# Expert products of a routed feed-forward layer, written as pairs of half-width products in TensorE's columns

## The chip, the cores and the metric

The kernel runs on one core of one Trainium2 chip. The metric is the device time of one execution in microseconds (us). The kernel before takes 718.14 us, the median of three runs (717.37 to 718.94). Everything is kept in 32-bit floats except a few masks.

A few words on names. TensorE (PE in the profile) multiplies a *stationary* matrix, loaded first into its array of 128 rows and 128 columns, by a *moving* matrix that is streamed through. In the profile the load is a record LDWEIGHTS of the row "PEld", the stream a record MATMUL of the row "PE". A product that uses only part of the array is told by its size in the records: `128*64` is one that fills all 128 rows and 64 of the columns. Two such products, one in each half of the columns, can be under way at the same time. PSUM is the memory that TensorE writes; the half of the columns used is the half of PSUM's 128 partitions written. VectorE is DVE, ScalarE is ACT, GpSimd is POOL, SyncE is SP.

## The reference, cut to what matters

First a block-sparse attention over 4 x 8 heads of 768 tokens gives `x`, 3072 rows of 512. Then each row goes to one of eight experts (the one whose embedding is nearest in angle), and is multiplied by that expert's two matrices:

```python
N, D, E, F = (3072, 512, 8, 1024)
...
expert_idx = np.argmax(logits, axis=1)
...
for e in range(E):
    mask = expert_idx == e
    ...
    h = np.maximum(x[mask] @ w1[e], 0.0)          # [rows, 512] @ [512, 1024]
    out[mask] = gate_w[mask, None] * (h @ w2[e])  # [rows, 1024] @ [1024, 512]
```

The change touches only these last two products.

## The kernel before

The attention comes first. Its products are 64 x 64 in size, four at a time in the four quarters of the array. Then the rows are grouped by expert into tiles of 128 rows. An *ordinary* tile belongs to one expert; a *mixed* tile holds 64 rows of one expert and 64 of another, and has always been written with `128*64` pairs. The program holds ordinary tiles under a condition on the number of tiles used, so that not all that are written run; in the profile 23 ordinary and 2 mixed tiles run.

The line numbers (L840 and so on) are those of the profile of the kernel before.

```python
P = 128; DM, E, F = 512, 8, 1024
ND, NF = DM // P, F // P          # 4, 8
HG = G // 2                       # 64

def prepare(k, i):                # turns the rows of the next tile
    ...
    for d in range(ND):
        k.nc.tensor.transpose(ps[:, d, :], x[:, d * P:(d + 1) * P], k.ident)      # L825, xg_ps
    k.turned_rows[i] = ring(k, "xgt", i, 2, k.wp, [P, ND, P])
    k.nc.vector.tensor_copy(out=k.turned_rows[i], in_=ps)

def expert_tile(k, i, meanwhile=None):                # an ordinary tile
    ...
    h = ring(k, "h", i, 2, k.wp2, [P, NF, P])
    half = NF // 2
    for f0 in (0, half):
        hp = ring(k, f"hp{f0}", i, 2, k.hps, [P, half, P])
        for f in range(half):
            for d in range(ND):
                nc.tensor.matmul(hp[:, f, :], lhsT=w1[:, d, (f0 + f) * P:(f0 + f + 1) * P], rhs=xt[:, d, :],
                                 start=(d == 0), stop=(d == ND - 1))              # L840
        if f0 == 0:
            nc.scalar.activation(h[:, 0:half], hp, ACT.Relu)                      # L843
            ...
        else:
            nc.vector.tensor_scalar(out=h[:, half:NF], in0=hp, scalar1=0.0, scalar2=None, op0=ALU.max)  # L847
    if i + 1 < NE + NL:
        prepare(k, i + 1)
    yp = ring(k, "yp", i, 1, k.eps, [P, DM])
    for f in range(NF):
        nc.tensor.matmul(yp, lhsT=h[:, f, :], rhs=w2[:, f, :], start=(f == 0), stop=(f == NF - 1))      # L853
    finish(k, i, yp, x, slot)     # scales the rows (DVE, L861) and scatters them to the output (POOL, L862)

def mixed_tile(k, i):                                 # not changed
    ...
    for f0 in (0, half):
        ...
        for d in range(ND):
            for s, (w1, _) in enumerate(weights):
                lanes = slice(HG * s, HG * (s + 1))
                nc.tensor.matmul(hp[lanes, :], lhsT=xt[:, d, lanes], rhs=w1[:, d, f0 * P:(f0 + half) * P],
                                 start=(d == 0), stop=(d == ND - 1))              # L881
    ...     # eight transposes to 128 x 128 (L893), with the four of prepare (L825) among them
    for f in range(NF):
        for s, (_, w2) in enumerate(weights):
            lanes = slice(HG * s, HG * (s + 1))
            nc.tensor.matmul(yp[lanes, :], lhsT=h[:, f, lanes], rhs=w2[:, f, :], start=(f == 0), stop=(f == NF - 1))  # L901
    finish(k, i, yp, x, slot)
```

`fetch` loads the weights of an expert (2 MB for each of its two matrices) into a ring of three buffers for each matrix, ahead of their use. Work left over from routing (ranks at L551 to L553, slots at L640, a count at L464) is put between and into the first expert tiles; its few products use all 128 columns.

Of the kernel before, what the change touches and what calls it, by code (L numbers as in the profile page):

```python
# [19 lines left out]
P = 128  # L20
# [9 lines left out]
ND, NF = DM // P, F // P  # L30
# [2 lines left out]
NE = (EARLY * S - E * (G - 1) + G - 1) // G  # L33
MIX = 2
HG = G // 2
NG = P // BLK
NU = N // G - NE

NL = max((N - NE * G - (HG + 1) * big - low) // G + big + max(low - 2 * MIX, 0) + (min(low, 2 * MIX) + 1) // 2
         for big in range(E + 1) for low in range(E + 1 - big))  # L40
# [208 lines left out]
def load_blocks(k, g, part=None):  # L249
# [5 lines left out]
    for n, src in enumerate((k.k, k.q)):  # L255
        for e in range(NG):
            src_e = src[b, 2 * j + e // 2].rearrange("(n t) (f d) -> f t n d", t=BLK, d=BLK)[e % 2]
# [428 lines left out]
def dispatch_late(k):  # L686
# [13 lines left out]
    nc.vector.scalar_tensor_tensor(out=low, in0=full, scalar=-float(G), in1=cnt, op0=ALU.mult, op1=ALU.add)  # L700
    nc.vector.tensor_scalar(out=low, in0=low, scalar1=-float(HG), scalar2=None, op0=ALU.is_le)
    half = tiny(name="half_e")
# [33 lines left out]
    nc.vector.scalar_tensor_tensor(out=move, in0=end, scalar=float(G), in1=lim, op0=ALU.mult, op1=ALU.subtract)  # L736
    nc.vector.tensor_scalar(out=there, in0=half, scalar1=float(HG), scalar2=-float(HG), op0=ALU.mult, op1=ALU.add)
    nc.vector.scalar_tensor_tensor(out=there, in0=end, scalar=-float(G), in1=there, op0=ALU.mult, op1=ALU.add)
# [16 lines left out]
def ring(k, name, i, n, pool, shape):  # L755

    key = name, i % n
    if key not in k.rings:
        k.rings[key] = pool.tile(shape, F32, name=f"{name}_{i % n}")
    return k.rings[key]  # L760
# [56 lines left out]
def prepare(k, i):  # L817

    x = k.rows[i][0]
    if i == 0:  # L820
        ps = two_banks(k, "first")[:, 0].rearrange("p (d t) -> p d t", d=ND)
    else:
        ps = ring(k, "xg_ps", i, 1, k.eps, [P, ND, P])
    for d in range(ND):
        k.nc.tensor.transpose(ps[:, d, :], x[:, d * P:(d + 1) * P], k.ident)  # L825
    k.turned_rows[i] = ring(k, "xgt", i, 2, k.wp, [P, ND, P])
    k.nc.vector.tensor_copy(out=k.turned_rows[i], in_=ps)


def expert_tile(k, i, meanwhile=None):  # L830
    nc = k.nc
    ((w1, w2),), (x, slot) = k.weights.pop(i), k.rows.pop(i)
    xt = k.turned_rows.pop(i)
# [3 lines that stand above are left out]
        hp = ring(k, f"hp{f0}", i, 2, k.hps, [P, half, P])  # L837
        for f in range(half):
            for d in range(ND):
                nc.tensor.matmul(hp[:, f, :], lhsT=w1[:, d, (f0 + f) * P:(f0 + f + 1) * P], rhs=xt[:, d, :],  # L840
                                 start=(d == 0), stop=(d == ND - 1))
        if f0 == 0:
            nc.scalar.activation(h[:, 0:half], hp, ACT.Relu)  # L843
            if meanwhile:
                meanwhile()
# [4 lines that stand above are left out]
        prepare(k, i + 1)  # L850
    yp = ring(k, "yp", i, 1, k.eps, [P, DM])
    for f in range(NF):
        nc.tensor.matmul(yp, lhsT=h[:, f, :], rhs=w2[:, f, :], start=(f == 0), stop=(f == NF - 1))  # L853
    finish(k, i, yp, x, slot)


def finish(k, i, yp, x, slot):

    nc = k.nc
    y = ring(k, "y", i, 2, k.wp2, [P, DM])  # L860
    nc.vector.tensor_scalar(out=y, in0=yp, scalar1=x[:, DM:XW], scalar2=None, op0=ALU.mult)  # L861
    nc.gpsimd.indirect_dma_start(  # L862
        out=k.out[:, :], out_offset=bass.IndirectOffsetOnAxis(ap=slot, axis=0),
        in_=y[:, :], in_offset=None, bounds_check=N - 1, oob_is_err=False,
    )


def mixed_tile(k, i):
# [7 lines left out]
    for f0 in (0, half):  # L876
        hp = ring(k, f"hp{f0}", i, 2, k.hps, [P, half, P]).rearrange("p f t -> p (f t)")
# [4 lines that stand above are left out]
# [16 lines left out]
# [4 lines that stand above are left out]
# [122 lines left out]
def expert_tiles(n, between=(), first=None):  # L1024
    between = iter(between)
    for i in range(NE + NU):
        if i + 2 == NE:
            for _ in between:
                pass
        fetch(n, i)  # L1030
        if len(parts(i)) == 2:
            mixed_tile(n, i)
        else:
            expert_tile(n, i, first if i == 0 else None)
        next(between, None)
    used = n.nc.values_load(n.used[0:1, 0:1], min_val=0, max_val=NL)
    with ExitStack() as more:
        for i in range(NU, NL):
            more.enter_context(n.tc.If(used > i))
            fetch(n, NE + i)  # L1040
            expert_tile(n, NE + i)
# [125 lines left out]
```

## Time and profile before

| what | number |
|---|---|
| time, median of three runs | 718.14 us |
| the profiled execution, first to last instruction | 719.4 us |
| TensorE clock granted, mean share | 0.987 |
| stretch of the attention | to about 339 us |
| stretch of the expert tiles | about 339 to 707 us |
| LDWEIGHTS records of TensorE | 8308 |
| HBM read, written | 147.62 MB, 16.01 MB |

The profile was taken in an execution of its own, so its span differs a little from the median. A product of 32-bit floats stands in it as two records LDWEIGHTS and two records MATMUL: the first product of an ordinary tile, written as 2 x 4 x 4 = 32 calls, has 64 of each. [...]the distance between the starts of two records, not the duration, is what a product costs in a stream of them. The chain of work that ended last (followed back from the last instruction, at each step to what released it) gives the time that each group added.

### The profile page before, as it was taken

The page shows a single profiled execution, that of the slowest core. Times are in us where ns is not written, and L with a number is a line of the kernel's source. Part 1 is how long each engine was busy: PE and PEld are TensorE (multiplying, and loading weights), DVE is VectorE, ACT ScalarE, POOL GpSimd, SP SyncE. Part 2 cuts the span into 40 slices and gives each one's busy share as a digit, 9 for nine tenths or more (in the row PEclk, how much of TensorE's full clock was granted, in tenths as well). Part 3 has the DMA queues.
Part 4 walks back from the last instruction along what each step waited for, and adds up shares of the span by engine and source line. Part 5 has one row for each costly group of instructions (what it writes and reads, how often), then busy time and mean ns, then how long its engine had stood idle before and what let it go on. Part 6 is the DMA issues. An engine that isn't in the chain of part 4 may idle for free.

```text
span 719.4 us, 19421 instructions
## 1 busy us (share of the span) xinstructions
PE 698.3 (97%) x8308; PEld 447.8 (62%) x8308; DVE 335.0 (47%) x683; ACT 188.5 (26%) x266; POOL 229.0 (32%) x385
## 2 busy tenths in 40 slices
PE   7899999999999999999999999999999999999992
PEld 3585555555555455556777677766576665767771
DVE  6677778777788888776582111111111111111110
ACT  4355554454545544554100000000000000000000
POOL 2225547554754547653601111111111121111110
PEclk9899999999999999999999999999999999999997
DMA  6433333365335947642999998998899998999980
GB/s 111 91 67 69 69 68 68 64 154 113 52 69 126 181 99 224 201 136 82 328 316 400 397 337 325 342 338 303 297 396 398 398 347 305 404 397 401 340 321 23
DMA packets 180808, 164.76 MB, mean 229 GB/s; under 512 B 128284, under 2 KB 128284, under 8 KB 180710
## 3 DMA queue, kind: packets, MB, share of 16 engines
q1 hardware_dynamic: 174950, 149.80, 66.6%
q0 software_dynamic: 4160, 13.39, 4.7%
q8 instruction: 69, 1.13, 0.7%
q10 hardware_dynamic: 1600, 0.20, 0.2%
q14 instruction: 29, 0.24, 0.1%
HBM read 147.62 MB, written 16.01 MB: 227 GB/s over the span
## 4 chain that ended last, share of the span: by engine, by line
PE 87%; DVE 4%; issue 3%; POOL 1%; DMA 1%; ACT 1%; SPq 1%; DVEq 0%; POOLq 0%; ACTq 0%
PE hp L840 21%; PE yp L853 21%; PE sc L353 19%; PE av L374 16%; PE back L409 3%; PE hp L881 2%; PE yp L901 2%; PE back L402 1%; PE xg_ps L825 1%; ACT e L356 1%; DVE kt L269 1%; DVE esum L371 1%; DVE at L380 0%; DMA out_dram<-y,slot_l 0%; DMA kld<-in_k_dram 0%
## 5 line engine op out<-in xcount | busy, mean ns | idle before, releaser
L356 ACT ACTIVATE e<-sc 128x768 f32<-128x768 f32 x192 | 155.7, 811 | 161.5 <-PE sc L353 156.3
L840 PEld LDWEIGHTS hp<-xgt,w 128*128 128x128 f32 x1472 | 167.7, 192 | 10.8 <-issue 10.2
L840 PE MATMUL hp<-xgt,w 128*128 128x128 f32 x1472 | 169.1, 275 | 0.0
L353 PE MATMUL sc<-qt,kt 64*64 64x384 f32 x1536 | 167.6, 489 | 0.0
L374 PE MATMUL av<-e,vld 64*64 64x384 f32 x1536 | 162.1, 491 | 2.3 <-DVE at L380 2.0
L853 PE MATMUL yp<-w,h 128*128 128x512 f32 x368 | 162.0, 593 | 0.1
L371 DVE TENSOR_TENSOR esum<-esum,e 128x768 f32<-128x768 f32 x128 | 130.9, 1023 | 44.0 <-ACT e L356 42.2
L853 PEld LDWEIGHTS yp<-w,h 128*128 128x128 f32 x368 | 68.0, 190 | 77.5 <-issue 76.3
L437 POOL TENSOR_TENSOR sq<-sq 128x192 f32<-128x192 f32 (+1 forms) x186 | 103.2, 555 | 13.9
L862 POOL DMA_INDIRECT out_dram<-y,slot_l x20 | 20.2, 1009 | 246.0 <-DVE y L861 233.9
L374 PEld LDWEIGHTS av<-e,vld 64*64 64x64 f32 x1536 | 58.6, 134 | 58.7 <-issue 26.7
L843 ACT ACTIVATE h<-hp 128x512 f32<-128x512 f32 x23 | 13.7, 597 | 298.3 <-PE hp L840 284.4
L353 PEld LDWEIGHTS sc<-qt,kt 64*64 64x64 f32 x1536 | 64.7, 135 | 37.3 <-issue 34.2
L861 DVE TENSOR_SCALAR y<-yp,xg 128x512 f32<-128x512 f32 x25 | 18.8, 750 | 140.7 <-PE yp L853 128.2
L847 DVE TENSOR_SCALAR h<-hp 128x512 f32<-128x512 f32 x23 | 15.9, 691 | 131.3 <-PE hp L840 131.3
L353 PE MATMUL sc<-qmask,kmask 64*64 64x384 bf16 x768 | 71.6, 327 | 1.0 <-DVE qmask L167 1.0
L433 POOL TENSOR_TENSOR sq<-x 128x384 f32<-128x384 f32 x31 | 27.0, 873 | 121.7 <-DVE part L422 108.5
L353 PEld LDWEIGHTS <-kmask 64*64 64x64 bf16 x768 | 27.9, 108 | 32.2 <-issue 31.3
L369 DVE TENSOR_TENSOR esum<-e 128x768 f32<-128x768 f32 x32 | 31.1, 973 | 11.5 <-ACT e L356 10.8
L409 PE MATMUL back<-ones,esum 64*64 64x1 f32 x1536 | 27.5, 192 | 0.0
L409 PEld LDWEIGHTS back<-ones,esum 64*64 64x64 f32 x1536 | 26.6, 137 | 0.0
L780 POOL DMA_INDIRECT xg<-x_dram,slot_l x22 | 22.6, 1026 | 6.7 <-issue 6.7
(193 smaller groups left out, 364.1 us busy)
## 6 DMA issues: line engine op xcount, KB each, us to landing
w<-in_moe_w_dram SPq DMA_DIRECT2D x54, 2048.0 KB
w<-in_moe_w_dram SPq DMA_DIRECT2D x16, 512.0 KB
x_dram<-x SPq DMA_DIRECT2D x24, 256.5 KB
vld<-in_v_dram SPq DMA_DIRECT2D x32, 192.0 KB
kld<-in_k_dram SPq DMA_DIRECT2D x60, 96.0 KB
qld<-in_q_dram SPq DMA_DIRECT2D x60, 96.0 KB
x_early<-x SPq DMA_DIRECT2D x12, 256.5 KB
ticks<-dens SPq DMA_DIRECT2D x32, 0.0 KB
```

What stands on the lines that cost most here:

```text
L353: nc.tensor.matmul(ps[D * r:D * (r + 1), h, 0:HALF], lhsT=rows[D * h:D * (h + 1), keys], rhs=cols[D * h:D * (h + 1), queries], start=first ...
L356: k.exps = nc.scalar.activation(e, ps[:, :, 0:HALF], ACT.Exp, scale=SCALE)
L369: k.summed = nc.vector.tensor_tensor(out=k.esum, in0=k.first, in1=e, op=ALU.add)
L371: k.summed = nc.vector.tensor_tensor(out=k.esum, in0=k.esum, in1=e, op=ALU.add)
L374: nc.tensor.matmul(k.av[D * h:D * (h + 1), r, 0:HALF], lhsT=v[D * r:D * (r + 1), h, kc, :], rhs=e[D * r:D * (r + 1), h, :], start=(kc == 0 ...
L409: nc.tensor.matmul(sums[D * s:D * (s + 1), t, h, r:r + 1], lhsT=esum[D * r:D * (r + 1), h, cols], rhs=k.ones[D * r:D * (r + 1), 0:1], star ...
L433: nc.gpsimd.tensor_tensor(out=sq, in0=x, in1=x, op=ALU.mult)
L437: k.squared = nc.gpsimd.tensor_tensor(out=out, in0=sq[:, :, 0:width], in1=sq[:, :, width:2 * width], op=ALU.add).ins
L780: k.nc.gpsimd.indirect_dma_start(out=x[:, :], out_offset=None, in_=(k.x_dram if late else k.x_early)[:, :], in_offset=bass.IndirectOffsetO ...
L840: nc.tensor.matmul(hp[:, f, :], lhsT=w1[:, d, (f0 + f) * P:(f0 + f + 1) * P], rhs=xt[:, d, :], start=(d == 0), stop=(d == ND - 1))
L853: nc.tensor.matmul(yp, lhsT=h[:, f, :], rhs=w2[:, f, :], start=(f == 0), stop=(f == NF - 1))
L862: nc.gpsimd.indirect_dma_start(out=k.out[:, :], out_offset=bass.IndirectOffsetOnAxis(ap=slot, axis=0), in_=y[:, :], in_offset=None, bounds ...
```

## The change: half-width pairs in ordinary tiles

Each product of an ordinary tile that filled the array with 128 stationary columns becomes two products of 64 stationary columns, which write the lower and the upper half of the partitions of the same PSUM tile. The moving operand is the same for both. It is meant to let the two halves of the array load and multiply independently of each other, so that a stationary operand of half the width is loaded in each half at the same time. The mixed tiles, the transposes, the loads of weights and the other engines' work are as they were.

```diff
 HG = G // 2
+SIDES = (slice(0, HG), slice(HG, P))
...
         for f in range(half):
             for d in range(ND):
-                nc.tensor.matmul(hp[:, f, :], lhsT=w1[:, d, (f0 + f) * P:(f0 + f + 1) * P], rhs=xt[:, d, :],
-                                 start=(d == 0), stop=(d == ND - 1))
+                for lanes in SIDES:
+                    nc.tensor.matmul(hp[lanes, f, :], lhsT=w1[:, d, (f0 + f) * P:(f0 + f + 1) * P][:, lanes],
+                                     rhs=xt[:, d, :], start=(d == 0), stop=(d == ND - 1))
...
     for f in range(NF):
-        nc.tensor.matmul(yp, lhsT=h[:, f, :], rhs=w2[:, f, :], start=(f == 0), stop=(f == NF - 1))
+        for lanes in SIDES:
+            nc.tensor.matmul(yp[lanes, :], lhsT=h[:, f, lanes], rhs=w2[:, f, :], start=(f == 0), stop=(f == NF - 1))
```

## The prediction, made before the changed kernel ran

> **What bounds the kernel now.** I read the page first: the engines' shares, then the costliest groups.
>
> ```profile
> PE 698.3 (97%) x8308; PEld 447.8 (62%) x8308; DVE 335.0 (47%) x683; ACT 188.5 (26%) x266; POOL 229.0 (32%) x385
> L840 PEld LDWEIGHTS hp<-xgt,w 128*128 128x128 f32 x1472 | 167.7, 192 | 10.8 <-issue 10.2
> L840 PE MATMUL hp<-xgt,w 128*128 128x128 f32 x1472 | 169.1, 275 | 0.0
> L853 PE MATMUL yp<-w,h 128*128 128x512 f32 x368 | 162.0, 593 | 0.1
> ```
>
> TensorE is never idle (97%), and the two changed products had next to no idle time before them (0.0 and 0.1 us). The second row is the interesting one: in the first product the loads of the stationary operand are busy 167.7 us, as long as the multiplying. Whichever of the two is the slower sets the pace.
>
> Next the chain that ended last, in order of time: first an ordinary tile, then the surroundings of a mixed tile. Columns: start, length, what, how many records.
>
> ```profile
> 443.86 7.14 PE hp L840 x64
> 451.01 0.44 PE xg_ps L825 x4
> 451.44 6.87 PE yp L853 x16
> ...
> 494.80 6.87 PE yp L853 x16
> 501.66 7.02 PE hp L881 x32
> 508.68 0.59 PE hp L893 x4
> 509.27 0.44 PE xg_ps L825 x4
> 509.70 0.45 PE hp L893 x4
> 510.16 7.02 PE yp L901 x32
> 517.18 7.34 PE hp L840 x64
> ```
>
> An ordinary tile is 7.14 + 0.44 + 6.87 = 14.45 us of TensorE without a gap. The stretch from 356 to 692 us of the chain holds nothing but TensorE, so a nanosecond won or lost there is won or lost in the time. The mixed tile is a measurement of the changed form, made by the kernel before: L901 is letter for letter what L853 becomes.
>
> Last, the timeline: of the weight loads at the start of the mixed tile, and of small products in the attention (columns: start, length from the first start to the last end, what).
>
> ```profile
> 501.59 0.20 PEld L881 LDWEIGHTS hp<-w,xgt 128*64 128x64 f32 x4 [0.76 <-issue]
> 502.08 0.14 PEld L881 LDWEIGHTS hp<-w,xgt 128*64 128x64 f32 x2 [0.28 <-issue]
> 502.51 0.14 PEld L881 LDWEIGHTS hp<-w,xgt 128*64 128x64 f32 x2 [0.29 <-issue]
> ```
> ```profile
> 201.04 0.56 PE L402 MATMUL back<-back,at 64*64 64x72 f32 x24
> 201.42 0.82 PE L409 MATMUL back<-ones,esum 64*64 64x1 f32 x48
> 202.09 0.85 PE L374 MATMUL av<-e,vld 64*64 64x384 f32 x8
> ```
>
> Two loads of 64 columns take 0.14 us together, and one alone 137 ns (the trace's duration): they run side by side, and the pairs follow each other every 0.43 us. The 24 products of 72 moving columns, six groups of four, take 201.42 - 201.04 = 0.38 us; the single starts in the trace put 62.5 ns between groups.
>
> **Two laws from these.** *Stream*: 6.87 us / 16 = 429.4 ns for 512 moving columns, and a transpose of 128 columns, 109.2 ns from start to start in the trace. So (429.4 - 109.2) / 384 = 0.834 ns for a column, and 429.4 - 512 x 0.834 = 2.4 ns on top. For 72 columns it gives 62.4; four quarters at once have 62.5. So tiles in parallel lose nothing in the stream. *Load*: groups of four with one moving column (L409) start 58.3 ns apart in the trace, which 64 loaded columns must set; the first product of an ordinary tile has 7.14 us / 64 = 111.6 ns with 128 loaded columns. Twice the columns, 53.3 ns more: 0.833 ns for a column, and 5 ns on top. So the first product is bound by its own weight loads, 111.6 against a stream of 109.2, by a hair; the second, at 429 ns with the same load under it, by its stream.
>
> **What the Trainium skill says.** "TensorE: Matmul & The Clock Gate", section "LDWEIGHTS (loading the stationary operand)", gives columns / 1.2 ns: 53.3 and 106.7, the slope measured here, without the 5 ns. Section "The mechanism" of that page says that a load overlaps with products under way only when the row groups differ; the trace contradicts it, as the two halves of L881 share all 128 rows and load and multiply side by side. "TensorEngine Tiling (Array Packing)", section "Key Properties", says that tiles load and multiply in parallel (the trace agrees) and that changing the tiling mode drains TensorE. The trace shows that too, and I take the price from it. The same page's "Restrictions" says that column tiling excludes the transpose mode for 32-bit floats; the transposes stay 128 wide in this kernel anyway.
>
> **The change part by part.**
>
> *The first product, faster.* Each half loads 64 columns (58.3 ns) under a stream of 128 (109.2 ns), so the stream becomes the pace: 64 steps x (111.6 - 109.2) = 0.15 us less per tile, 6.99 us. This is the whole possible gain, 23 x 0.15 = 3.5 us.
>
> *The second product, the same.* 16 pairs at 429 ns; L901 shows this pace.
>
> *Changes of mode, new.* The transposes between the two products are 128 wide, so each ordinary tile now leaves the paired mode and enters it again. Prices from the chain: entering costs 7.02 - 6.87 = 0.15 us (the same 16 steps, L881 or L901 against L853). Leaving into transposes costs 0.59 - 0.44 = 0.15 (L893 after L881 against four undisturbed transposes). Leaving into an ordinary first product costs 7.34 - 7.14 = 0.20. From one tile's second product to the next tile's first there is no change of mode. So +0.30 per tile.
>
> *Sum per tile*: 6.99 + 0.59 + 7.02 = 14.60 against 14.45, +0.15 us; x 23 = +3.4 us.
>
> *At the edges.* The mixed tiles no longer change the mode where they meet ordinary ones: 2 x (0.15 + 0.20) = 0.7 us less. Three pieces of routing with 128-wide products (L551 to L553 after the first tile, L640 before and L464 inside a later first product) now stand amid paired work: 3 x 0.30 = 0.9 us more. Net +0.2.
>
> *Beside the path.* DVE's ReLU of the second half (0.69 us) is needed by the fifth of eight steps of the second product, 4 x 0.86 us after its start. So it stays hidden. Weight transfers are the same. The sum is +3.6 us: 718.14 + 3.6 = 721.7 us.
>
> **Rivals.**
>
> *Only the gain.* If leaving a 128-column stream cost nothing, because less is under way than in L881's 512-column one, the time would be about 718.14 - 3.5 = 714.6. Against it: the second group of four transposes in the mixed tile (L893, 0.45) is itself a stream of 128 columns, and L901 behind it still pays 0.15.
>
> *TensorE's dispatch becomes the bound.* Records double: 1472 + 368 = 1840 more of each kind, and the first product asks for a load and a multiply every 54.6 ns for 7 us. For it: no stretch of the profile runs 128-row pairs with so short a stream. Against it: the attention's unit of 20 loads and 20 multiplies takes 1.45 us, 73 ns each, over 330 us, and L402 and L409 have 72 of each in 1.05 us, 14.5 ns each, which shows the rate in bursts only. A pace of 62 ns per record pair instead of 54.6 would make it 64 x 15 ns x 23 = 22 us more, 740 us: slower by 3%.
>
> *The two loads of a pair hinder each other*, as the section quoted would have it. Then 2 x 58.3 = 117 ns per step bind: 64 x (117 - 109.2) x 23 = +11 us, 733 us. The 0.14 us for two loads speaks against it, though under a stream of 512 columns.
>
> *Weight transfers come late.* In the window from 520 to 570 us the DMA engines were busy throughout at 393 GB/s, while TensorE did not wait. An ordinary tile needs 4.2 MB in 14.45 us, 290 GB/s. A tile that takes longer only eases this. No change in the time.
>
> **Range and chances.** The prices were read off at this same clock and repeat at both mixed tiles (they are +7.1 us of the sum, the faster pace is -3.5). What I extrapolate is the pace of the 128-column pairs: 1 ns there is 1.5 us. That gives 719.0 to 726.0, with a thin tail up to the two slower rivals and hardly any below. Chances: faster 0.02, within 2% 0.93, slower 0.05.
>
> **What would show it.** In the changed profile: the chain should have 23 blocks of about 7.0 (128 records), 0.59 (4) and 7.02 us (32), adding up to 14.60; the first product's starts should come 109 ns apart in pairs with 6 or 7 ns within a pair; its loads' mean duration should fall from 192 to some 137 ns. The first product after a mixed tile should lose its extra 0.20. I am wrong if the first product is over 7.2 us (a rival of pace) or the transposes keep 0.44 (no price for leaving). I am also wrong if idle time turns up before TensorE's rows.

## The result, and the profile after

The changed kernel takes 723.75 us (median of six runs, 720.79 to 723.98), the kernel before in the same series 719.13 us. The ratio is 1.006, with a 95% interval from 1.004 to 1.0079: 0.6% slower, about 4.3 us (2.9 to 5.7) of 719.13. The two medians themselves differ by 4.6 us; here and below a difference in us that stands beside a ratio is worked out from that ratio. Run again in another series it gave 1.0069 (1.005 to 1.0088). The prediction was 721.7 us from 718.14, +3.6 us, a ratio of 1.005. Of the 2 us between 721.7 and 723.75, 1 us is the median of the kernel before, which moved from 718.14 to 719.13 with three more runs.

From the page of the changed kernel, the engines' shares and the two changed products (L842 is the first, L856 the second; below, L826 are the transposes, and L884, L896 and L904 the products and transposes of a mixed tile):

```profile
PE 700.5 (97%) x10148; PEld 424.4 (59%) x10148; DVE 333.5 (46%) x683; ACT 188.5 (26%) x266; POOL 228.0 (32%) x385
L842 PEld LDWEIGHTS hp<-xgt,w 128*64 128x64 f32 x2944 | 162.2, 137 | 12.1 <-issue 11.4
L842 PE MATMUL hp<-xgt,w 128*64 128x128 f32 x2944 | 165.4, 273 | 0.0
L856 PE MATMUL yp<-w,h 128*64 128x512 f32 x736 | 163.2, 595 | 0.3 <-DVE h L849 0.3
```

Each of the two products has twice its records, and TensorE is as full as before. A load takes 137 ns instead of 192. Yet the busy time of the loads (162.2 us) hides what was gained: it counts any time with a load under way, and with pairs there nearly always is one. The chain in order of time tells more. An ordinary tile, then a mixed one:

```profile
443.87 6.99 PE hp L842 x128
450.86 0.59 PE xg_ps L826 x4
451.44 7.02 PE yp L856 x32
...
495.21 7.02 PE yp L856 x32
502.23 6.87 PE hp L884 x32
509.10 0.59 PE hp L896 x4
509.69 0.44 PE xg_ps L826 x4
510.12 0.46 PE hp L896 x4
510.58 7.02 PE yp L904 x32
517.60 6.99 PE hp L842 x128
```

The first product fell from 7.14 to 6.99 us; the transposes rose from 0.44 to 0.59, the second product from 6.87 to 7.02. A tile takes 14.60 us instead of 14.45. Beside the mixed tile the old prices are gone: its first product (L884) takes 6.87 instead of 7.02, and the ordinary product behind it 6.99 instead of 7.34.

Where the time went, from the single starts in the traces ("attention" is up to the first expert product, "experts" from there to the start of the last record of a second product, "end" from there to the last instruction):

| trace | attention | experts | end | span |
|---|---|---|---|---|
| before | 338.98 | 366.91 | 13.47 | 719.4 |
| after | 337.22 | 370.23 | 14.34 | 721.8 |
| after, again | 338.27 | 370.26 | 14.31 | 722.8 |

The experts take 3.3 us more, at a granted TensorE clock of 1.00 in the traces of before and after alike. The attention scatters by itself: 335.4 to 339.0 us over the traces of before, after, after again and the five variants with changed pairs or transposes and all tokens. The end is 0.85 us longer in both traces of the changed kernel, which no term of the prediction had. The sum of the two, 4.2 us, agrees with the 4.3 us of the ratio.

### The profile page after: what moved, and what is told of

It is laid out like the page before. It is cut to its first block, busy times and chain, and to the rows that moved or that the text cites. A ratio compares the mean times of both kernels' runs of the same rounds, so it can differ in the third digit from the quotient of the medians.

```text
span 721.8 us, 23101 instructions
## 1 busy us (share of the span) xinstructions
PE 700.5 (97%) x10148; PEld 424.4 (59%) x10148; DVE 333.5 (46%) x683; ACT 188.5 (26%) x266; POOL 228.0 (32%) x385
## 4 chain that ended last, share of the span: by engine, by line
PE 88%; DVE 4%; issue 3%; POOL 1%; DMA 1%; ACT 1%; SPq 0%; DVEq 0%; POOLq 0%; ACTq 0%
PE yp L856 21%; PE hp L842 20%; PE sc L354 20%; PE av L375 16%; PE back L410 3%; PE yp L904 2%; PE hp L884 2%; PE xg_ps L826 2%; PE back L403 1%; DVE kt L270 1%; DVE esum L372 1%; ACT e L357 1%; DVE at L381 0%; DMA vld<-in_v_dram 0%; DMA out_dram<-y,slot_l 0%
## 5 line engine op out<-in xcount | busy, mean ns | idle before, releaser
L842 PEld LDWEIGHTS hp<-xgt,w 128*64 128x64 f32 x2944 | 162.2, 137 | 12.1 <-issue 11.4
L354 PE MATMUL sc<-qt,kt 64*64 64x384 f32 x1536 | 165.9, 490 | 0.0
L842 PE MATMUL hp<-xgt,w 128*64 128x128 f32 x2944 | 165.4, 273 | 0.0
L856 PE MATMUL yp<-w,h 128*64 128x512 f32 x736 | 163.2, 595 | 0.3 <-DVE h L849 0.3
L375 PE MATMUL av<-e,vld 64*64 64x384 f32 x1536 | 160.3, 491 | 2.1 <-DVE at L381 1.8
L856 PEld LDWEIGHTS yp<-w,h 128*64 128x64 f32 x736 | 50.7, 137 | 96.4 <-issue 95.3
```

The costliest lines, as they stand in the source:

```text
L354: nc.tensor.matmul(ps[D * r:D * (r + 1), h, 0:HALF], lhsT=rows[D * h:D * (h + 1), keys], rhs=cols[D * h:D * (h + 1), queries], start=first ...
L375: nc.tensor.matmul(k.av[D * h:D * (h + 1), r, 0:HALF], lhsT=v[D * r:D * (r + 1), h, kc, :], rhs=e[D * r:D * (r + 1), h, :], start=(kc == 0 ...
L842: nc.tensor.matmul(hp[lanes, f, :], lhsT=w1[:, d, (f0 + f) * P:(f0 + f + 1) * P][:, lanes], rhs=xt[:, d, :], start=(d == 0), stop=(d == ND ...
```

## The experiments

My theory was a price for each change between paired and full-width products, against a small gain in the pace of a load-bound product. The rivals were a price for each paired product, loads that hinder each other, and a limit of dispatch.

**Each product alone.** Only the first product in pairs:

```diff
     for f in range(NF):
-        for lanes in SIDES:
-            nc.tensor.matmul(yp[lanes, :], lhsT=h[:, f, lanes], rhs=w2[:, f, :], start=(f == 0), stop=(f == NF - 1))
+        nc.tensor.matmul(yp, lhsT=h[:, f, :], rhs=w2[:, f, :], start=(f == 0), stop=(f == NF - 1))
```

> Only the first product in pairs; the second is 128 wide again. Theory (a price for each change between paired and full-width products, 0.15 us to enter and 0.15 or 0.20 to leave; a pace of 109.2 ns instead of 111.6 in the first product): the tile still changes twice, so 7.14 (6.99 + 0.15 for entering), 0.59 and 6.87 us in the chain, 14.60 in all, and 3.3 us over the kernel before. Rival (the 0.15 us belong to each paired product, not to the change): 6.99 or 7.14, 0.44 or 0.59 and 6.87, no entering price after the full-width second product.

Its chain:

```profile
456.66 7.14 PE hp L842 x128
463.80 0.58 PE xg_ps L826 x4
464.39 6.87 PE yp L855 x16
```

7.14 + 0.58 + 6.87 = 14.59, ratio 1.004 (1.0029 to 1.0051), about 2.9 us. The price of entering has moved from the second product to the first, as expected. The second product alone in pairs:

```diff
             for d in range(ND):
-                for lanes in SIDES:
-                    nc.tensor.matmul(hp[lanes, f, :], lhsT=w1[:, d, (f0 + f) * P:(f0 + f + 1) * P][:, lanes],
-                                     rhs=xt[:, d, :], start=(d == 0), stop=(d == ND - 1))
+                nc.tensor.matmul(hp[:, f, :], lhsT=w1[:, d, (f0 + f) * P:(f0 + f + 1) * P], rhs=xt[:, d, :],
+                                 start=(d == 0), stop=(d == ND - 1))
```

> Only the second product in pairs. Theory (a price for each change): 7.34 us for the first product, which follows a paired one (leaving costs 0.20 there), 0.44 for the transposes, 7.02 for the second product; 14.80 a tile, some 7.2 us over the kernel before, slower than the whole change although less is changed. Rival (0.15 us for each paired product): 7.14, 0.44, 7.02, some 3.4 us over the kernel before.

```profile
444.22 7.34 PE hp L841 x64
451.56 0.44 PE xg_ps L826 x4
452.00 7.02 PE yp L855 x32
```

14.80 us a tile, ratio 1.0096 (1.006 to 1.0132), about 6.9 us. The first product, whose code is that of the kernel before, became 0.20 us slower because of what stands ahead of it. So the price is not one of the paired products themselves.

**Twice as many changes.** The same work as the changed kernel, but the transposes split, two after each half of the first product; and the same split in the kernel before:

```diff
-def prepare(k, i):
+def prepare(k, i, some=range(ND)):
...
-    for d in range(ND):
+    for d in some:
         k.nc.tensor.transpose(ps[:, d, :], x[:, d * P:(d + 1) * P], k.ident)
+    if ND - 1 not in some:
+        return
...
             if meanwhile:
                 meanwhile()
+            if i + 1 < NE + NL:
+                prepare(k, i + 1, range(ND // 2))
...
-        prepare(k, i + 1)
+        prepare(k, i + 1, range(ND // 2, ND))
     yp = ring(k, "yp", i, 1, k.eps, [P, DM])
```

> The whole change, and the four transposes of a tile split into two after the first half of the first product and two after the second half: the same work, twice as many changes between paired and full width. Theory (a price for each change): 0.30 us more per tile than the changed kernel, 14.89 a tile, about 10.5 us over the kernel before. Rival (the price belongs to the paired products, or to waiting for their results): no more than the changed kernel, 3.5 to 4.5 us over the kernel before.

> The kernel before with the same split of the transposes, all at full width. Every theory of the change: within 0.5 us of the kernel before, as no mode changes. If it were slower by several us, the split itself costs and the run with pairs says less.

The chain of the paired one, then of the full-width one:

```profile
401.12 3.49 PE hp L844 x64
404.62 0.37 PE xg_ps L826 x2
404.98 3.64 PE hp L844 x64
408.63 0.37 PE xg_ps L826 x2
409.00 7.02 PE yp L860 x32
```
```profile
397.19 3.57 PE hp L842 x32
400.76 0.22 PE xg_ps L825 x2
400.98 3.57 PE hp L842 x32
404.56 0.22 PE xg_ps L825 x2
404.77 6.87 PE yp L857 x16
```

Paired, the four places behind a change pay 0.15 us each (0.37 against 0.22 twice, 3.64 against 3.49, 7.02 against 6.87): 14.89 us a tile, ratio 1.015 (1.012 to 1.018), 10.8 us. At full width nothing is paid: ratio 1.0004 (0.9991 to 1.0016). The price doubles with the changes at equal work, so it belongs to the change.

**No change within a tile.** The transposes as paired plain products with the identity:

```diff
     for d in range(ND):
-        k.nc.tensor.transpose(ps[:, d, :], x[:, d * P:(d + 1) * P], k.ident)
+        for lanes in SIDES:
+            k.nc.tensor.matmul(ps[lanes, d, :], lhsT=x[:, d * P:(d + 1) * P][:, lanes], rhs=k.ident,
+                               start=True, stop=True)
```

> The whole change, and the transposes of ordinary rows also as pairs of 64 columns, as plain products with the identity (two passes instead of one, so they take twice their stream). No change of mode is left in an ordinary tile. Theory (a price for each change): 6.99, 8 steps x 109.2 = 0.87 and 6.87 us, 14.73 a tile; with the mixed tiles, which now change amid their transposes, about 8 us over the kernel before. Rival (the price belongs to the paired products): 0.30 more per tile, 15.03, about 14 us over.

Here pairs of neighbouring groups interlock, so the chain mixes their borders:

```profile
398.96 6.98 PE hp L844 x126
405.94 0.01 PE xg_ps L827
405.94 0.10 PE hp L844
406.05 0.77 PE xg_ps L827 x14
406.81 6.87 PE yp L858 x32
413.68 6.98 PE hp L844 x126
```

From 398.96 to 413.68 a tile takes 14.72 us, expected 14.73, with the second product at 6.87 although paired. The ratio is 1.0117 (1.0093 to 1.014), 8.4 us: no change is paid for, but the transposes, in two passes instead of one, cost 0.43 us more, above the 0.30 saved.

The traces agree with the ratios of all four paired variants: from the first expert product to the last instruction they are 2.8, 6.7, 10.3 and 8.0 us longer than before, in the order above, beside 2.9, 6.9, 10.8 and 8.4 us by the ratios.

**Loads against streams.** To see which of them binds the first product, I took half of the stream away in both forms. These two kernels leave out half of the tokens in the first product (tokens 64 to 127 take the results of 0 to 63), so only its blocks are read:

```diff
-                nc.tensor.matmul(hp[:, f, :], lhsT=w1[:, d, (f0 + f) * P:(f0 + f + 1) * P], rhs=xt[:, d, :],
+                nc.tensor.matmul(hp[:, f, 0:HG], lhsT=w1[:, d, (f0 + f) * P:(f0 + f + 1) * P], rhs=xt[:, d, 0:HG],
                                  start=(d == 0), stop=(d == ND - 1))
...
-            nc.scalar.activation(h[:, 0:half], hp, ACT.Relu)
+            nc.scalar.activation(h[:, 0:half].rearrange("p f (r t) -> p f r t", r=2),
+                                 hp[:, :, 0:HG].unsqueeze(2).broadcast_to([P, half, 2, HG]), ACT.Relu)
```

(the ReLU of the second half likewise, and the paired form with `lanes`).

> The kernel before, its first product streaming 64 of the 128 tokens only (the other 64 are left out and take the same results). Theory (128 loaded columns take 111.6 ns and bind the first product): 7.14 us stay as they are, though half of the stream is gone. Rival (the stream binds, and a full-width product has 2.4 ns more of its own): 64 x (64 x 0.834 + 5) = 3.7 us.

> The changed kernel with the same 64 of 128 tokens in its first product. Theory (64 columns load in 58.3 ns, both halves at once): 64 x 58.3 = 3.73 us, half of the full-width one. Rival 1 (loads of two halves in the same rows hinder each other): 64 x 111.6 to 117 = 7.1 to 7.5 us. Rival 2 (TensorE's dispatch has its limit between 29 and 54 ns for a load and a multiply): between 3.9 and 6.9 us.

The timeline, full width and then paired (start, length from the first start to the last end):

```profile
425.46 7.25 PE L840 MATMUL hp<-xgt,w 128*128 128x64 f32 x64
432.56 0.61 PE L825 MATMUL xg_ps<-ident,xg 128*128 128x128 f32 x4
```
```profile
414.59 3.90 PE L842 MATMUL hp<-xgt,w 128*64 128x64 f32 x128
418.42 0.66 PE L826 MATMUL xg_ps<-ident,xg 128*128 128x128 f32 x4
```

At full width, taking away half of the stream changes almost nothing: 432.56 - 425.46 = 7.10 us, 111 ns a step. The loads bind. In pairs it is 418.42 - 414.59 = 3.83 us, of which 0.10 belong to leaving; the chain gives the product 3.73, 58.3 ns a step, as much as the groups of 64 x 64 loads in the attention took. So the loads of the two halves do run side by side. The Trainium skill ("TensorE: Matmul & The Clock Gate", section "The mechanism") says that a load overlaps with products under way only when their row groups differ; it does not speak of two loads. Here both halves use the same 128 rows, and two loads and two products fit into 58.3 ns, so the measurement decides against it. TensorE also takes a load and a multiply every 29 ns for 3.7 us, so dispatch is far from a limit at 54.6.

The whole times of these two (739.7 and 677.08 us, one run each) are not compared. In the trace of the full-width one the order of instructions is another too: some transposes stand a tile earlier and wait for their rows. In the paired one, tiles of 11.3 us outrun the weights. The waits, full width and then paired (us in total, times, longest):

```profile
PE xg_ps L825 <- DMA xg<-x_dram,slot_l: 9.8, 4, 3.9
PE hp L886 <- DMA w<-in_moe_w_dram: 7.4, 2, 5.9
```

The mixed tiles of the paired one, which need two experts' weights, wait for them, with the DMA engines at 398 GB/s.

**The end.** To see whether the extra 0.85 us belong to the pairs or to where the last branches lie in TensorE's stream of instructions, 32, 64 or 96 products were put at the very start:

```diff
         k.nc.tensor.matmul(ps[:, 0], lhsT=k.zeros[:, 0:P], rhs=k.zeros, start=True, stop=True)
+    for i in range(32):
+        k.nc.tensor.matmul(ps[:, 0, 0:8], lhsT=k.zeros[:, 0:P], rhs=k.zeros[:, 0:8], start=True, stop=True)
```

> The changed kernel with 32 products of 8 moving columns more at the very start, to move all later instructions of TensorE to other places in its instruction stream. Looked at: the end, from the start of the last product to the last instruction (13.5 us before, 14.3 in both traces of the changed kernel, 13.5 and 13.7 in two others of its paired variants). Theory (where the last branches fall in the instruction stream): 13.5 to 13.7 in at least one of the three shifts, with TensorE's branch there at some 0.8 us instead of 3.1 after that start. Rival (the paired form in both products lengthens the end): 14.3 in all three.

> As the run with 32, with 64 such products. The two theories expect the same of it as of that one: an end of 13.5 to 13.7 us in at least one shift, or 14.3 in all.

> As the run with 32, with 96 such products. The two theories expect the same of it as of that one: an end of 13.5 to 13.7 us in at least one shift, or 14.3 in all.

> The kernel before with 64 such products at the start. Theory (place in the instruction stream): its end can lengthen as well, to 14.3 us, or stay at 13.5. Rival (the paired form): 13.5 us.

The ends are 13.59, 13.49 and 13.48 us in the changed kernel, and 13.64 in the kernel before with 64. The experts stay at 370.24 to 370.26 us in the three shifted ones. TensorE's branch past the tiles that don't run is the last of three of its line; before, after, and after with 64 products more (PEldq is TensorE's sequencer; shortest, median and longest in ns, then the first and the last start):

```profile
L1037 PEldq COMPARE_BRANCH  x3: 86/193/4234, 686.1 to 706.7; - x3
L1040 PEldq COMPARE_BRANCH  x3: 86/312/3725, 689.6 to 710.5; - x3
L1042 PEldq COMPARE_BRANCH  x3: 86/200/3371, 688.4 to 707.0; - x3
```

The last products start at 705.89, 707.45 and 706.24 us. The branch comes 0.78 us after that start in the kernel before, 0.79 in all three shifted ones, and 3.07 and 3.16 in the two traces of the changed kernel. GpSimd's last branch, which begins at 3.9 us in all of them, takes 3.4 to 3.5 us up to GpSimd's next instruction in the changed kernel, and 2.6 to 2.8 in the kernel before and the shifted ones. In the changed kernel another branch of TensorE runs during the whole of it, from 4.0 to 8.2 us; in those that branch has ended by 5.5 us. Whether this overlap is what lengthens GpSimd's branch is not shown.

So the 0.85 us do not belong to the paired form: the same pairs end without them once the instructions are moved. Why TensorE's branch is late in the unmoved kernel remains open. Two other kernels have as many MATMUL records as the changed one, 10148: the paired one with half of the tokens is late too (2.73 us, an end of 17.59), the one with split transposes is not (0.79 us, 13.54). So the number of records alone does not decide it. The whole times, of one run each, do not show the end: 721.5, 721.54 and 724.02 us with 32, 64 and 96 products, 717.08 us for the kernel before with 64 and 717.09 without, and the attention took 335.95, 335.98 and 338.50 us in the traces of the first three.

**The changed kernel again**

> The changed kernel once more, on the same chip as the three others, for a closer interval. The trace of TensorE has 3.3 us more from the first expert product to the last; theory: 3.3 to 3.6 us over the kernel before (0.5%). If it is clearly over 4.5 us, something outside of the expert products is slower too.

Ratio 1.0069, 5.0 us. That is over the 4.5 named, though not clearly, as the interval goes from 3.6 to 6.3 us. Its trace shows what is slower outside of the experts: the end, by 0.84 us.

## Why the prediction was right

- *What binds*: right. TensorE alone; next to no idle time came in ahead of the two products (0.0 and 0.3 us in all).
- *The first product faster by 0.15 us*: right, 6.99 us, starts 109 ns apart with 7 ns within a pair. That it had been bound by its loads at 111.6 ns was argued from two groups of records; the halved stream shows it (7.10 us with 64 columns moving, 7.14 with 128).
- *The second product the same, plus entering*: right, 7.02 us. Alone in pairs it brings nothing and costs 0.35 us a tile.
- *The prices, 0.15 to enter, 0.15 or 0.20 to leave*: right to 0.01 us, in four arrangements. Leaving into the transposes costs as much after 128 or 64 moving columns (0.59 and 0.58 us) as after 512 (0.59 in the mixed tile), so the first rival falls. What TensorE does in that time no run shows; shown is that the change costs it.
- *The sum per tile*: 14.60 as predicted. Over 23 tiles, 14.592 - 14.450 = 0.142 us each by single starts, 3.3 us.
- *The edges, +0.2*: measured +0.1 (3.33 in all for the experts, less 3.27 for the tiles). The mixed tiles save 0.7 us as predicted; by the chains the routing costs some 0.7 instead of 0.9.
- *The total*: +3.6 predicted, +4.3 measured in the first series, +5.0 in the second. The step that lacks is the end. The prediction took everything behind the last tile to be as before; it was 0.85 us longer, which is not a cost of the pairs. With intervals of almost 3 us the total alone would prove little; the blocks of the chain do.
- *The two slower rivals* (dispatch; loads that hinder each other): excluded by 58.3 ns a step. The 62 ns that the prediction tried for the dispatch rested on no measurement; 29 ns were reached. *Late weight transfers*: not at 14.6 us a tile, but they come in at 11.3.
- *Not in the prediction*: the program's own instructions are transferred too, and with more records there are more of them. In the queue below (packets, MB, share of the engines' time) it is 69 packets before and 84 after, 72 with the second product alone in pairs and 80 with the first. No idle time of TensorE came of it: from 356 to 707 us it was busy for 351.00 of 351 us.

```profile
q8 instruction: 69, 1.13, 0.7%
q8 instruction: 84, 1.38, 0.8%
```

None of the runs is a faster kernel. An estimate from these prices: if the transposes of two tiles were done together, two tiles would pay 0.30 us for one leaving and one entering and gain 2 x 0.15 us in their first products, just even. It was not tried.

## What to carry to other kernels

Dividing a product that fills TensorE into column halves did not speed up its stream here (16 pairs with 512 moving columns took 6.87 us behind paired work, like 16 whole products); it only halved the columns of each load. So look first at which of the two sets the distance between starts (here 111.6 ns by loads against 109.2 by the stream, in one product of two). Then count the changes between tilings that the division brings: each cost 0.15 to 0.20 us here, as much as the whole gain of a product with 64 steps. Where the program already mixes both forms, the chain shows these prices at the borders before anything is changed.

## What was not expected

A change that left GpSimd's instructions alone lengthened the end by 0.85 us, while TensorE's branch past unused tiles came 2.3 us later; 32 small products at the start of the program took both away again. A difference of this size between two builds need not come from the change that is studied. And the loads' time has a constant part: 58.3 ns for 64 columns and 111.6 for 128 make 0.833 ns a column and 5 ns on top. Two points fix such a line and do not test it; but four quarters with one moving column and two halves with 64 have the same 58.3 ns.
